# Attention and FFN on one core: scores of two heads at once on the two halves of the array's rows

## The chip, the cores and the metric

The kernel runs on one core of a Trainium2 chip. The metric is the device time of one execution in microseconds (us), taken as the median of several runs. Engines are named as in the profile: PE is TensorE (PEld its weight loads), DVE is VectorE, ACT is ScalarE, POOL is GpSimd, SP issues the DMAs of this kernel.

## The reference

The inputs are q, k and v of shape (4, 8, 576, 64) (batch, heads, sequence, head size), and the two weights of a feed-forward layer.

```python
q_rot, k_rot = rotate(q), rotate(k)                       # rotary embedding over the head size
scores = matmul(q_rot, k_rot^T) / sqrt(64)
attn = exp(scores - max(scores)) ; attn /= sum(attn) + 1e-9
x = (attn @ v), heads joined                               # 2304 tokens x 512
h = x @ w_in                                               # 512 -> 2048
out = (h * clip(h + 3, 0, 6) / 6) @ w_out                  # 2048 -> 512
```

The weights arrive as 64-bit floats and are decoded on the chip. The factors of the data are large, so the kernel keeps nearly the accuracy of f32: nearly every operand is split into a high and a low f16 part, and products are sums of several f16 matmuls.

## The kernel before, in words

**Tiles.** The 2304 tokens are 18 tiles of 128. A batch has 4.5 tiles, so tiles 4 and 13 are mixed: their upper 64 tokens belong to one batch and their lower 64 to the next (`BAT`, line 26). Tile 0 goes a way of its own in f32 (`attention_first`). For the other 17 tiles, each of the 8 heads is one unit `attention(i)` (line 637), with i = 8 t + h.

**One head.** `emit_qk` (line 600) computes 128 x 576 scores into a PSUM tile S of two banks (288 columns in each). There are two buffers of S. The q of a head lies in `qT` as 128 rows: 64 rows of the high part over 64 of the low part; k lies in `kT` in the same way. So one matmul over 128 rows gives high x high + low x low, and a second one, with a copy of q whose halves are swapped, gives the two cross products: two matmuls for each bank, four a head, with the full array. In a mixed tile each of these is two matmuls, one for each half of the tokens, on 64 columns of the array each (line 611). DVE then scales S in place and takes the maximum (line 655), ACT takes the exponential in place in S with the sum (line 657), ACT or DVE writes its high f16 part to P in SBUF (lines 664, 666), and DVE the low part (line 668). Only then is S free. A DMA transpose turns P into PT (line 674), and `emit_av` (line 614) multiplies PT with the parts of v, 14 matmuls of 64 columns. After the eight heads `emit_x` (line 818) normalises the tile, and a transpose hands it to the FFN (`ffn_h`, line 871, and `ffn_o`, line 937), which works on blocks of one or two tiles, with three f16 products for every f32 one.

**Preparation.** `prep_q` (line 340) loads a tile of q, bounds it (ACT or DVE), rotates it (lines 277 to 282, on POOL mostly), splits it into q1 (high and low of each head side by side; the low part is line 302), copies it with the halves swapped to q2 (line 357, DVE), and transposes both by DMA (lines 362 and 364). `prep_k` (line 377) and `prep_v` (line 443) do the like for a batch of keys and values. `decode_w` (line 520) turns 64-bit words of the weights into f32: one pass for the magnitude (line 528, ACT), one for the low word (line 541 on POOL, 543 on ACT), one for the sign (line 549 on ACT), one that joins them (line 555, DVE). `split_w_steps` splits the result.

**The order.** The order of every engine's instructions is written when the kernel is built. Each piece of work is a generator that yields what it needs next: an engine and an estimated time ("D" for DVE, "A", "P", "E" for PE), a DMA ("S" plain, "Z" transpose), a buffer ("R"), a condition ("C"). A small planner, `Emission` (line 41), keeps a clock of these estimates, gives each engine the waiting piece of the lowest priority number, and emits instructions in that order; on the chip each engine then runs its own list strictly in order. Some steps may go to one of several engines (`yield "Xeh", {...}`): the planner takes the cheapest by its clock and a bias. Small letters ("d") and "P" mark work that takes the port to SBUF that DVE and POOL share, by the planner's model. The dictionary `CFG` (line 38) holds the priorities and biases. Attention comes ahead of the FFN by priority, but `attn_ready` (line 758) holds a head back until enough FFN units are done (`lead`). The planner counts 0.5 us of PE for the scores of one head:

```python
yield "R", "S"
yield "E", 0.5
S = psum.tile([128, 2, 512], F32, tag="S", bufs=2, name="S")
emit_qk(i, S)
```

## Time and profile before

| | us |
|---|---|
| median of 3 runs | 659.03 |
| lowest and highest run | 657.67, 661.57 |
| the profiled execution, its own time | 654.6 |
| span of its instructions | 652.7 |

A page of the profile shows the busy time of each engine, the span in 40 slices and the groups of instructions; views of the trace answer for a stretch, a line or a tile. Busy PE is not PE at its peak: a matmul is shown from its start to its end, and matmuls in a row overlap, so the time that a matmul takes from its neighbours is read from the distance of starts, not from its length. In the timeline, instructions of one line in a row are merged to one row with its start and its count.

### The profile page before, as it was taken

How to read it: one execution, taken by the hardware profiler on the slowest of the kernel's cores; microseconds unless marked ns; L12 is line 12 of the kernel's file. 1: busy time of each engine (PE TensorE's matmuls, PEld its weight loads, DVE VectorE, ACT ScalarE, POOL GpSimd, SP SyncE). 2: the span in 40 equal slices, each digit the busy share in tenths (PEclk: the TensorE clock that was granted, in tenths of full speed). 3: DMA queues.
4: the chain of work that ended last, by engine and by line, in shares of the span. 5: the costliest groups of instructions: out<-in, count | busy, mean ns of one | idle time of the engine just before them, and what ended most of it. 6: DMA issues, size and time to landing. Idle time of an engine off the chain costs nothing.

```text
span 652.7 us, 14935 instructions
## 1 busy us (share of the span) xinstructions
PE 573.3 (88%) x5860; PEld 410.8 (63%) x5860; DVE 447.6 (69%) x844; ACT 386.2 (59%) x715; POOL 322.2 (49%) x363
## 2 busy tenths in 40 slices
PE   2478888468899999898998999999999999999997
PEld 1366764256576766675776756766677677666663
DVE  6899889999975986688697787765777656311010
ACT  4875988655775766667577667664667656312110
POOL 3574535597433795634499441562544524233330
PEclk9989799569999999999999999999999999999999
DMA  9995394976979998998996999777699756310000
GB/s 300 320 322 135 138 262 101 194 138 119 207 157 143 209 162 146 179 168 170 201 158 133 186 203 163 135 143 144 109 158 175 134 113 106 74 33 17 17 1 33
DMA packets 252294, 97.96 MB, mean 150 GB/s; under 512 B 235840, under 2 KB 235968, under 8 KB 252224
## 3 DMA queue, kind: packets, MB, share of 16 engines
q1 hardware_dynamic: 252224, 97.01, 73.5%
q8 instruction: 46, 0.75, 0.5%
q14 instruction: 24, 0.20, 0.1%
HBM read 31.97 MB, written 4.72 MB: 56 GB/s over the span
## 4 chain that ended last, share of the span: by engine, by line
PE 52%; POOL 14%; DVE 11%; DMA 9%; issue 7%; ACT 6%; SPq 1%; POOLq 0%; DVEq 0%; ACTq 0%
PE o L963 20%; PE h L901 17%; DMA PT<-P 6%; PE av L626 5%; PE S L608 5%; POOL ropeA L277 3%; POOL kst L280 3%; POOL kst L282 3%; DVE P L668 2%; DVE S L655 2%; PE S L697 2%; DVE tg L922 1%; PE S L611 1%; PE av L747 1%; DMA raw<-in_w_out 1%
## 5 line engine op out<-in xcount | busy, mean ns | idle before, releaser
L901 PEld LDWEIGHTS <-wi_st 128*128 128x128 f16 x1920 | 164.7, 98 | 55.3 <-issue 3.4
L963 PE MATMUL o<-wo_st,g 128*128 128x512 f16 x696 | 186.2, 379 | 2.8 <-ACT wo_st L983 1.6
L901 PE MATMUL h<-wi_st 128*128 128x256 f16 (+1 forms) x1344 | 162.3, 259 | 1.1 <-DVE tg L922 0.7
L657 ACT ACTIVATE S<-S,mx 128x576 f32<-128x576 f32 x136 | 96.9, 713 | 100.9 <-DVE S L655 99.1
L655 DVE TENSOR_SCALAR_CACHE_REDUCE S<-S,sig 128x576 f32<-128x576 f32 x136 | 109.6, 819 | 31.1 <-PE S L608 25.3
L668 DVE SCALAR_TENSOR_TENSOR P<-S,P 128x576 f16<-128x576 f32 x136 | 100.9, 752 | 31.7 <-ACT P L664 31.2
L294 POOL TENSOR_SCALAR g<-tg 128x512 f16<-128x512 f32 x44 | 28.0, 637 | 182.0 <-DVE tg L922 172.3
L922 DVE SCALAR_TENSOR_TENSOR tg<-tg,h 128x512 f32<-128x512 f32 x68 | 46.5, 683 | 89.3 <-ACT tg L915 89.3
L626 PEld LDWEIGHTS <-PT 128*128 128x128 f16 (+1 forms) x2128 | 74.2, 103 | 42.7 <-DMA PT<-P 26.1
L915 ACT ACTIVATE tg<-h,g,block_sc 128x512 f32<-128x512 f32 x68 | 52.8, 776 | 79.5 <-PE h L901 70.8
L963 PEld LDWEIGHTS <-g 128*128 128x128 f16 x696 | 64.9, 98 | 44.5 <-POOL g L932 6.9
L608 PE MATMUL S<-kT,qT 128*128 128x288 f16 x480 | 79.9, 297 | 13.4 <-DVE P L668 13.1
L664 ACT ACTIVATE P<-S 128x576 f16<-128x576 f32 x135 | 85.6, 647 | 1.8
L626 PE MATMUL av<-vA,PT 128*128 128x64 f16 (+1 forms) x1520 | 64.9, 197 | 21.1 <-DMA PT<-P 20.1
L932 POOL TENSOR_TENSOR g<-tg,g 128x512 f16<-128x512 f32 x58 | 67.4, 1162 | 8.8 <-ACT g L290 5.3
L901 PE MATMUL h<-xTa,wi_st 128*128 128x256 f16 (+1 forms) x576 | 68.4, 255 | 0.0
L608 PEld LDWEIGHTS <-qT 128*128 128x128 f16 x480 | 44.8, 101 | 33.7 <-DVE P L668 17.4
L626 PE MATMUL av<-vB,PT 128*128 128x64 f16 (+1 forms) x608 | 39.4, 196 | 0.0
L963 PE MATMUL o<-wo_st 128*128 128x512 f16 x120 | 32.7, 380 | 2.3 <-POOL wo_st L294 1.3
L277 POOL TENSOR_TENSOR ropeA<-kst,rope_sb 128x512 f32<-128x512 f32 (+1 forms) x16 | 20.9, 1308 | 13.7 <-DMA kst<-in_k 13.0
L841 POOL TENSOR_TENSOR x<-x,x 128x512 f16<-128x512 f32 x15 | 18.3, 1217 | 17.9 <-ACT x L290 17.9
L657 ACT ACTIVATION_READ_ACCUMULATOR S<-S,mx 128x1 f32 x136 | 26.6, 196 | 0.0
(150 smaller groups left out, 761.9 us busy)
## 6 DMA issues: line engine op xcount, KB each, us to landing
raw<-in_w_in SPq DMA_DIRECT2D x16, 512.0 KB, 7.6
raw<-in_w_out SPq DMA_DIRECT2D x16, 512.0 KB, 4.6
qraw<-in_q SPq DMA_DIRECT2D x18, 256.0 KB, 3.2
out<-wo_st SPq DMA_DIRECT2D x17, 256.0 KB, 2.6
kst<-in_k SPq DMA_DIRECT2D x16, 256.0 KB, 4.3
vst<-in_v SPq DMA_DIRECT2D x15, 256.0 KB, 4.5
PT<-P SPq DMA_TRANSPOSE x136, 3.4
vB<-vA SPq DMA_DIRECT2D x8, 256.0 KB, 3.9
```

What stands on the lines that cost most here:

```text
L277: ENG[e].tensor_tensor(out=v4(ta), in0=x4[:, :, ::-1, :], in1=sinb.to_broadcast([n, 8, 2, 32]), op=ALU.mult)
L608: PE.matmul(out=S[:, j, 0:288], lhsT=qT_t[t][:, o, h, :], rhs=kT_t[b0][:, h, ks], **st)
L626: PE.matmul(out=av[r0:r1, h, :], lhsT=PT[:, blk, r0:r1], rhs=rhs, start=(n == 0), stop=(n == len(terms) - 1))
L655: DVE.tensor_scalar(out=E, in0=E, scalar1=sig_t[t], scalar2=3.0e38, op0=ALU.mult, op1=ALU.min, accum_out=mx)
L657: ACT.activation(out=E, in_=E, func=ACTF.Exp, scale=-1.0, bias=mx, accum_out=sum_t[t][:, h:h + 1])
L664: ACT.activation(out=hi, in_=E, func=ACTF.Copy, scale=ES)
L668: DVE.scalar_tensor_tensor(out=lo, in0=E, scalar=ES, in1=hi, op0=ALU.mult, op1=ALU.subtract)
L901: PE.matmul(out=h[:, i, :], lhsT=wi_h(p, wl)[:, 256 * c + f0:256 * c + f0 + 128], rhs=xT[:, 4 * xl + c, :], start=(n == 0), stop=(n == 11))
L915: ACT.activation(out=tg, in_=hf, func=ACTF.Relu, scale=osc[j], bias=g3)
L922: DVE.scalar_tensor_tensor(out=whole if j < NF else tg, in0=tg, scalar=6.0 * GAM, in1=hf, op0=ALU.min, op1=ALU.mult)
L932: ENG[e].tensor_tensor(out=gf[:, 1], in0=tg, in1=gf[:, 0], op=ALU.subtract)
L963: PE.matmul(out=os[n][0], lhsT=g[:, gl, mm % nm, 128 * n:128 * n + 128], rhs=wo_h(mm, wl), start=(mm == 0 and gl == 0 and wl == 0), stop=( ...
```

## The change

- Scores are computed for two heads at once. q is now laid out as 512 columns of high parts and then 512 of low parts; its transpose `qT` has 8 slices of 128 rows: slices 0 to 3 are the high parts of two heads each (64 rows a head), slices 4 to 7 the low parts. k is laid out in the same way.
- For each pair of heads there are three terms (high x high, high x low, low x high) instead of four; each is a matmul over 64 rows, on the upper half of the array's rows for the even head and on the lower half for the odd one. The two heads write to the two S buffers, so a pair takes both at once.
- The swapped copy of q and its transpose fall away; q16 and qT have half the size, q16 one buffer.
- The exponential may go to a new SBUF tile E (two buffers). The planner decides for each head: if an E is free and the shared port is free soon enough (`CFG["sb"]` of the phase). S is then free after the exponential, and the two parts of P are made from E; the high part on DVE is then estimated at 0.44 us.
- The low word of the weights is read as 16-bit words (its upper half) instead of 32-bit ones, by the same two engines; the planner's estimate for ACT falls from 1.35 to 1.15 us.
- The bounds of v and of the first weight may go to ACT as well as to DVE.
- The planner's numbers in `CFG` are all new (among them `lead` 32 to 29, `a16` 1 to 0, `gate` 1.71 to 2.284).

```diff
-LOW = 2.0 ** -29 * (1 - 2.0 ** -10), -0.5 + 7.5 * 2.0 ** -10
+LOW = 2.0 ** -13, -0.5 + 2.0 ** -14
...
+NE = 2
...
-        q1 = left.tile([128, 8, 2, 64], F16, tag="q16", bufs=2, name="q1")
-        bound(e, am, x, q1.rearrange("p h a d -> p (h a d)")[:, 0:512])
+        q16 = left.tile([128, 2, 512], F16, tag="q16", name="q16")
+        bound(e, am, x, q16[:, 0])
...
-        x3 = x.rearrange("p (h d) -> p h d", d=64)
-        yield from split_steps(x3, s, q1[:, :, 0, :], q1[:, :, 1, :])
-        yield "d", 0.41
-        q2 = left.tile([128, 8, 2, 64], F16, tag="q16", bufs=2, name="q2")
-        DVE.tensor_copy(out=q2, in_=q1[:, :, ::-1, :])
+        yield from split_steps(x, s, q16[:, 0], q16[:, 1])
...
-        qT = left.tile([128, 2, 8, 128], F16, tag="qT", bufs=2, name="qT")
-        SP.dma_start_transpose(out=qT[:, 0], in_=q1.rearrange("p h a d -> p (h a d)"))
-        yield "Z", 0.9
-        SP.dma_start_transpose(out=qT[:, 1], in_=q2.rearrange("p h a d -> p (h a d)"))
+        qT = left.tile([128, 8, 128], F16, tag="qT", bufs=2, name="qT")
+        SP.dma_start_transpose(out=qT, in_=q16.rearrange("p l n -> p (l n)"))
...
-            yield from split_steps(x3, sc[0][0:n], k16[0:n, :, 0, :], k16[0:n, :, 1, :])
+            yield from split_steps(kst[0:n, i], sc[0][0:n], k16[0:n, 0:512], k16[0:n, 512:1024])
...
-                yield "D", 0.67
-                bound("D", am[:, i:i + 1], vst[:, i])
+                e = yield "Xvb", {"D": 0.67, "A": 0.82}
+                bound(e, am[:, i:i + 1], vst[:, i], vA[:, 1, i])
...
+        upper = raw.bitcast(U16)[:, :, 1]
-        e = yield "Xlow", {"P": 1.35, "A": 1.35}
+        e = yield "Xlow", {"P": 1.35, "A": 1.15}
         if e == "P":
-            POOL.tensor_scalar(out=low, in0=raw[:, :, 0], scalar1=LOW[0], scalar2=LOW[1], op0=ALU.mult, op1=ALU.add)
+            POOL.tensor_scalar(out=low, in0=upper, scalar1=LOW[0], scalar2=LOW[1], op0=ALU.mult, op1=ALU.add)
...
-        e = "D" if kind == "i" else em.choose("wbo", {"D": 1.21, "A": 1.25}, 3)
+        e = em.choose("wb" + kind, {"D": 1.21, "A": 1.25}, 3)
...
     def emit_qk(i, S):
-        t, h = divmod(i, 8)
+        t, c = i // 8, i % 8 // 2
         b0, b1 = BAT[t]
-        for o in range(2):
+        groups = [(0, 128, b0)] if b0 == b1 else [(0, 64, b0), (64, 128, b1)]
+        terms = (0, 0), (0, 4), (4, 0)
+        for n, (lq, lk) in enumerate(terms):
             for j in range(2):
-                ks = slice(288 * j, 288 * j + 288)
-                st = dict(start=(o == 0), stop=(o == 1))
-                if b0 == b1:
-                    PE.matmul(out=S[:, j, 0:288], lhsT=qT_t[t][:, o, h, :], rhs=kT_t[b0][:, h, ks], **st)
...
+                for p in range(2):
+                    d = slice(64 * p, 64 * p + 64)
+                    for r0, r1, b in groups:
+                        PE.matmul(out=S[p][r0:r1, j, 0:288], lhsT=qT_t[t][d, lq + c, r0:r1],
+                                  rhs=kT_t[b][d, lk + c, 288 * j:288 * j + 288],
+                                  start=(n == 0), stop=(n == len(terms) - 1))
...
-        yield "R", "S"
-        yield "E", 0.5
-        S = psum.tile([128, 2, 512], F32, tag="S", bufs=2, name="S")
-        emit_qk(i, S)
+        if h % 2 == 0:
+            yield "R", "S"
+            yield "R", "S"
+            yield "E", 0.76
+            for p in range(2):
+                S_t[i + p] = psum.tile([128, 2, 512], F32, tag="S", bufs=2, name="S")
+            emit_qk(i, (S_t[i], S_t[i + 1]))
...
+        else:
+            yield "C", lambda: i in qk_done
+        S = S_t.pop(i)
...
+        in_sbuf = em.tokens["E"] > 0 and em.port - em.clock < CFG["sb"][em.phase]
+        if in_sbuf:
+            yield "R", "E"
         yield "A", 0.93
-        ACT.activation(out=E, in_=E, func=ACTF.Exp, scale=-1.0, bias=mx, accum_out=sum_t[t][:, h:h + 1])
+        if in_sbuf:
+            E = left.tile([128, 576], F32, tag="E", bufs=NE, name="E").rearrange("p (j n) -> p j n", j=2)
+        ACT.activation(out=E, in_=S[:, :, 0:288], func=ACTF.Exp, scale=-1.0, bias=mx, accum_out=sum_t[t][:, h:h + 1])
         yield "N", 0.0
+        if in_sbuf:
+            free("S")
...
-        e = yield "Xeh", {"A": 0.65, "D": 0.75}
+        e = yield "Xeh", {"A": 0.68, "d": 0.44} if in_sbuf else {"A": 0.65, "D": 0.75}
...
-        yield "D", 0.75
+        yield "d" if in_sbuf else "D", 0.75
...
-        free("S")
+        free("E" if in_sbuf else "S")
...
-                and (i == 0 or i - 1 in started) and units_done[0] >= i - CFG["lead"]
+                and (i % 2 or i - 1 in started) and units_done[0] >= i - CFG["lead"]
```

## Rows read from the trace of the kernel before

**Rows 1.** The page: busy us, share of the span and instructions of each engine, and the busy tenths of TensorE and its granted clock in 40 slices of the span.
```profile
PE 573.3 (88%) x5860; PEld 410.8 (63%) x5860; DVE 447.6 (69%) x844; ACT 386.2 (59%) x715; POOL 322.2 (49%) x363
...
PE   2478888468899999898998999999999999999997
...
PEclk9989799569999999999999999999999999999999
```

**Rows 2.** Busy time by stretch: the stretch and its length in us, then the busy us and instructions of each engine, the granted clock of TensorE, the share of the DMA engines and GB/s.
```profile
60.00:100.00 40.00, 33.73 (x230) 27.64 (x231) 34.30 (x50) 33.47 (x48) 16.50 (x13) 0.87 0.75 208
100.00:170.00 70.00, 48.86 (x534) 34.31 (x533) 67.04 (x112) 48.29 (x86) 44.78 (x44) 0.78 0.75 136
...
170.00:570.00 400.00, 380.97 (x4419) 273.34 (x4417) 287.53 (x599) 251.61 (x500) 204.81 (x244) 1.00 0.85 155
...
570.00:637.00 67.00, 65.24 (x451) 43.44 (x449) 8.93 (x13) 12.67 (x17) 24.14 (x27) 1.00 0.06 17
637.00:652.70 15.70, 11.40 (x52) 4.99 (x52) 0.00 (x0) 1.37 (x2) 0.10 (x1) 1.00 0.09 34
```

**Rows 3.** Waits of TensorE's matmuls from 170 to 570 us: who waited for whom, us in total, times, longest us.
```profile
PE av L626 <- DMA PT<-P: 10.3, 11, 2.5
PE S L608 <- DVE P L668: 3.3, 5, 1.3
PE o L963 <- ACT wo_st L983: 1.6, 1, 1.6
```

**Rows 4.** The timeline of TensorE around the scores of two heads of an unmixed tile (full array): start in us, length to the end of the last one, line, operation, array rows x columns, shape, count.
```profile
387.72 0.81 PE L963 MATMUL o<-wo_st 128*128 128x512 f16 x3
388.36 1.14 PE L608 MATMUL S<-kT,qT 128*128 128x288 f16 x8
389.34 0.46 PE L626 MATMUL av<-vA,PT 128*128 128x64 f16 x10
```

**Rows 5.** The same around the scores of two heads of a mixed tile (halves of the array's columns).
```profile
195.72 0.81 PE L963 MATMUL o<-wo_st 128*128 128x512 f16 x3
196.46 1.17 PE L611 MATMUL S<-kT,qT 128*64 128x288 f16 x16
197.56 0.34 PE L901 MATMUL h<-wi_st 128*128 128x128 f16 x3
```

**Rows 6.** The same around the only matmuls of the kernel that use half of the array's rows (transposes of 64 keys in f32).
```profile
26.18 0.69 PE L320 MATMUL xt<-id_sb,kst 64*128 64x64 f32 x4 [6.43 <-DVE kst L282]
26.80 2.07 PE L697 MATMUL S<-wi_st,xTa 128*128 128x288 f32 x4
```

**Rows 7.** Score matmuls before and after 170 us, line 608 (full array) and then line 611 (halves of columns): stretch, length, busy us and count of the matmuls and of the weight loads, clock, DMA.
```profile
0.00:170.00 170.00, 18.66 (x92) 9.28 (x92) 0.87 0.80 201
170.00:653.00 483.00, 61.25 (x388) 35.52 (x388) 1.00 0.72 132
...
170.00:653.00 483.00, 10.47 (x128) 6.12 (x128) 1.00 0.72 132
```

**Rows 8.** The timeline of TensorE around the scores of single heads of a mixed tile.
```profile
187.42 0.68 PE L611 MATMUL S<-kT,qT 128*64 128x288 f16 x8 [0.23 <-DVE P L668]
188.03 0.68 PE L901 MATMUL h<-wi_st 128*128 128x128 f16 x9
188.75 0.68 PE L611 MATMUL S<-kT,qT 128*64 128x288 f16 x8
189.36 0.34 PE L901 MATMUL h<-wi_st 128*128 128x128 f16 x3
```

**Rows 9.** The tile q: line, engine and operation with count, duration in ns (min/median/max), first and last start in us, shapes. SPq is the queue that issues the DMAs.
```profile
L362 SPq DMA_TRANSPOSE qT<-q x17: 1232/1305/2063, 46.6 to 519.2; - x17
L357 DVE COPY q<-q x17: 409/420/823, 47.1 to 518.8; 128x1024 f16<-128x1024 f16 x17
L364 SPq DMA_TRANSPOSE qT<-q x17: 1322/1339/2657, 49.9 to 524.9; - x17
```

**Rows 10.** The tile S, with the same columns.
```profile
L655 DVE TENSOR_SCALAR_CACHE_REDUCE S<-S,sig x136: 804/820/828, 64.0 to 559.8; 128x576 f32<-128x576 f32 x136
L655 DVE DVE_READ_ACCUMULATOR S<-S,sig x136: 130/141/145, 64.8 to 560.6; 128x1 f32 x136
L657 ACT ACTIVATE S<-S,mx x136: 668/715/725, 71.9 to 560.7; 128x576 f32<-128x576 f32 x136
...
L668 DVE SCALAR_TENSOR_TENSOR P<-S,P x136: 739/751/759, 78.3 to 562.3; 128x576 f16<-128x576 f32 x136
L664 ACT ACTIVATE P<-S x135: 630/651/677, 73.3 to 561.6; 128x576 f16<-128x576 f32 x135
...
L712 ACT ACTIVATE E<-S,bi x8: 724/732/776, 31.0 to 60.4; 128x576 f32<-128x576 f32 x8
```

**Rows 11.** Line 302, the low split with both operands in SBUF, with the same columns.
```profile
L302 DVE SCALAR_TENSOR_TENSOR q<-qraw,qs,q x17: 732/752/1631, 45.8 to 518.0; 128x512 f16<-128x512 f32 x17
L302 DVE SCALAR_TENSOR_TENSOR k<-kst,ks,k x15: 736/1172/1748, 133.2 to 371.9; 128x512 f16<-128x512 f32 x12, 64x512 f16<-64x512 f32 x3
```

**Rows 12.** VectorE's costliest groups from 100 to 170 us: line, operation, shapes, count, busy us, mean ns, idle before in us.
```profile
L655 DVE TENSOR_SCALAR_CACHE_REDUCE S<-S,sig 128x576 f32<-128x576 f32 x17 | 13.7, 814 | 0.0
L668 DVE SCALAR_TENSOR_TENSOR P<-S,P 128x576 f16<-128x576 f32 x18 | 13.3, 748 | 0.7 <-ACT P L664 0.7
...
L357 DVE COPY q<-q 128x1024 f16<-128x1024 f16 x2 | 0.8, 418 | 0.0
```

**Rows 13.** Lines 541 (low words of the weights) and 549 (signs), with the columns of rows 9.
```profile
L541 POOL TENSOR_SCALAR wo_st<-raw x8: 1346/1422/2315, 16.5 to 57.2; 128x1024 uint16<-128x1024 uint32 x8
L541 POOL TENSOR_SCALAR tw<-raw x8: 1344/1358/1377, 64.4 to 97.3; 128x1024 uint16<-128x1024 uint32 x8
...
L549 ACT ACTIVATE tw<-raw x8: 1346/1364/1371, 69.5 to 101.2; 128x1024 f16<-128x1024 f32 x8
```

More of the change, by code (lines that the diff above doesn't have):

```diff
@@ L194, in attention_ffn @@
     TT = {"d": 0.68, "P": 1.265}
[L195 removed]
+    em = Emission({"S": 2, "E": NE, "P16": NP16, "PT": NPT, "av": 1, "x": 1, "h": 2, "tg": 2, "g": NG,
                    "o": 1, "ob": 1, "rope": 1, "rope0": 1, "k16": 1, "raw": 3, "raw1": NR1, "tw": 0, "tw0": 2, "rope1": 1})
@@ L417, in split @@
             n = N[i]
-            x3 = kst[0:n, i].rearrange("p (h d) -> p h d", d=64)
             if start is None:
                 yield "R", "k16"
-            k16 = left.tile([128, 8, 2, 64], F16, tag="k16", name="k16") if start is None else \
-                wo16[:, 8 + i].rearrange("p (h a d) -> p h a d", a=2, d=64)
-            yield from split_steps(x3, sc[0][0:n], k16[0:n, :, 0, :], k16[0:n, :, 1, :])
+            k16 = left.tile([128, 1024], F16, tag="k16", name="k16") if start is None else wo16[:, 8 + i]
+            yield from split_steps(kst[0:n, i], sc[0][0:n], k16[0:n, 0:512], k16[0:n, 512:1024])
             yield "Z", 0.9
             SP.dma_start_transpose(out=kT[0][:, :, 128 * i:128 * i + n],
-                                   in_=k16[0:n].rearrange("p h a d -> p (h a d)"))
+                                   in_=k16[0:n])
             yield "N", 0.0
@@ L538, in decode_w @@
         low, sign = h[:, :, 0].bitcast(U16), h[:, :, 1]
-        e = yield "Xlow", {"P": 1.35, "A": 1.35}
+        upper = raw.bitcast(U16)[:, :, 1]
+        e = yield "Xlow", {"P": 1.35, "A": 1.15}
         if e == "P":
-            POOL.tensor_scalar(out=low, in0=raw[:, :, 0], scalar1=LOW[0], scalar2=LOW[1], op0=ALU.mult, op1=ALU.add)
+            POOL.tensor_scalar(out=low, in0=upper, scalar1=LOW[0], scalar2=LOW[1], op0=ALU.mult, op1=ALU.add)
         else:
-            ACT.activation(out=low, in_=raw[:, :, 0], func=ACTF.Copy, scale=LOW[0], bias=LOW[1])
+            ACT.activation(out=low, in_=upper, func=ACTF.Copy, scale=LOW[0], bias=LOW[1])
         e = yield "Xsg", {"P": 1.34, "A": 1.15}
@@ L594, in split_w_steps @@
         wdone[kind] = done if kind == "i" else 2 * done + 1
[L597 removed]
+    PT_t, sum_t, av_t, S_t = {}, {}, {}, {}
     started, qk_done, done_av = set(), set(), set()
     def emit_qk(i, S):
[L601 removed]
+        t, c = i // 8, i % 8 // 2
         b0, b1 = BAT[t]
[L603 removed]
+        groups = [(0, 128, b0)] if b0 == b1 else [(0, 64, b0), (64, 128, b1)]
+        terms = (0, 0), (0, 4), (4, 0)
+        for n, (lq, lk) in enumerate(terms):
             for j in range(2):
[L605 to L612 removed]
+                for p in range(2):
[4 more added lines that the diff above has]
+                                  start=(n == 0), stop=(n == len(terms) - 1))
     def emit_av(i):
```

15 lines of the change are left out of this document (5 added, 10 removed).

## The prediction

> **What bounds the kernel now.** I read the page's shares first. TensorE is busy 88% of the span, VectorE 69%, and the slices show TensorE at 8 or 9 tenths from the tenth slice on [rows 1]. Because that share averages unlike stages, I next read the table by stage [rows 2]. Up to 170 us TensorE is far from full, and from 100 to 170 us VectorE is the bound: 67.04 of 70 us busy, while TensorE does 48.86 us at a mean clock of 0.78. From 170 to 570 us TensorE is busy 380.97 of 400 us at full clock, VectorE only 287.53, ScalarE 251.61, GpSimd 204.81. From there to the end TensorE still does 65.24 of 67 and 11.40 of 15.7 us. So after 170 us the time is TensorE's work plus about 19 us of idle before 570 us, and a microsecond taken from TensorE's work there comes off the end. The waits [rows 3] name that idle: 10.3 us for transposed exponentials (PT), 3.3 us for an S buffer that VectorE still reads. The forecast rests on this stage.
>
> **The array's time for scores.** A pair of heads is now 8 matmuls of 288 columns on the full array. Their first starts at 388.36 us and the next operation at 389.34, so a pair takes 0.98 us, 0.1225 us a matmul [rows 4]. The new pair is 12 matmuls of 64 rows. If the two halves of the rows run together, these are 6 slots of 0.1225, 0.735 us. No row shows two matmuls on row halves, but tiles 4 and 13, whose 128 tokens span two batches, run their scores on two halves of the *columns*. There 16 matmuls start at 196.46 and the next operation at 197.56 us: 1.10 us for 8 slots [rows 5], so halves of columns do run together, and the burst costs 0.12 us beyond 8 x 0.1225. Ahead of that burst, three matmuls on 512 columns take from 195.72 to 196.46, 0.74 us; ahead of the burst on the full array the same three take from 387.72 to 388.36, 0.64 us [rows 4, 5]. So going into the split form costs 0.10 us and coming out 0.12: 0.22 us a burst.
>
> I take this for row halves too. The nearest row on row halves is a group of four small f32 transposes on 64 rows, from 26.18 to 26.80 us, of which the merged line tells only that 0.62 us pass for four [rows 6]; it excludes neither a cost nor none. A pair is then 0.735 + 0.22 = 0.955 us, against 0.98. From 170 us on, 388 of the 480 full-array matmuls run, 97 heads or 48.5 pairs [rows 7]: 48.5 x 0.025 = **1.2 us saved**.
>
> All 128 split matmuls, 16 heads, also run after 170 us [rows 7]. A burst of 8 for one head takes 0.61 us (187.42 to 188.03, 188.75 to 189.36) [rows 8] and 0.10 us to enter: 16 x 0.71 = 11.4 us if each stood alone, 8 x 1.20 = 9.6 if all came in twos [rows 5]; I take 10.6. With four quarters at once, eight pairs cost 8 x 0.955 = 7.6: **3.0 us saved**. The sum for TensorE is 4.2 us. Its bounds: without any price for the change of form, 48.5 x 0.245 + 10.6 - 8 x 0.735 = 11.9 + 4.7 = 16.6 us saved; with halves that don't overlap, 12 x 0.1225 + 0.22 = 1.69 a pair, 48.5 x 0.71 = 34 us lost.
>
> The Trainium skill, "TensorEngine Tiling (Array Packing)", section Theoretical Speedup, gives up to 2x for a contraction of 64 or less, by which a pair would be 0.735 us and the sum 16.6 us; its Key Properties say that a change of tiling mode drains the engine, which speaks against a burst as short as this one. The rows on column halves agree with the drain, 0.22 us; on row halves no row decides, and I keep the drain.
>
> **The copy of q and its second transpose.** Removed are 17 copies on VectorE (420 ns median) and 17 transposes on the SP queue (1339 ns to issue), 22.8 us of that queue's time [rows 9]. After 170 us VectorE has slack, so the copy is worth nothing there; two of the copies lie in 100 to 170 us: 2 x 0.42 = 0.8 us. The queue passes 136 PT transposes, and the 10.3 us of waits for PT are where relief would show [rows 3]: between 0 and 10.3 us, and since 17 transposes go and the 136 PT ones stay, I take **1 us**. The waits for PT then go on, as the next thing late. The new layout of q16 and k16 moves no work: the splits write as many elements. q16 has one buffer in place of two, but a tile's preparation starts when the scores of the tile before are nearly done, long after its transpose, so nothing waits for it.
>
> **Exponentials in SBUF.** S now comes free after the exponential instead of after both split passes; today it is held for those, 651 + 751 ns more [rows 10]. But a pair takes both S buffers at once, so its scores wait for the later of two. The 3.3 us of waits for S can vanish or grow; I take no change (the rival below has the other price). The exponential itself moves from PSUM to SBUF: the eight of the first tile that already write to SBUF take 732 ns against 715 [rows 10], 17 ns more on ScalarE, which is 63% busy from 170 to 570 us: nothing. The low split on VectorE now reads two operands from SBUF. From PSUM it took 739 to 759 ns in all 136 cases [rows 10]; the like operation with both operands in SBUF has medians of 752 (q) and 1172 (k) and goes up to 1748 [rows 11]. So it can be held up while GpSimd works. SBUF is chosen by the planner's guess that the shared port is free, so I take q's median, nothing. At k's median it is 0.42 us a head: the 18 low splits from 100 to 170 us [rows 12], where VectorE is full, would cost 7.6 us; later its slack covers it.
>
> The Trainium skill, "SBUF — State Buffer", section Who interferes with whom, says that a VectorE instruction with two SBUF inputs contends with GpSimd's reads, which speaks against this part; the spread of the rows agrees. The page gives no time for this shape.
>
> **The weights' low words.** The 16 passes stand on GpSimd today (1422 and 1358 ns medians, all before 100 us) [rows 13]. Reading 16-bit words instead of 32-bit moves as many elements; GpSimd is busy 16.50 of 40 us from 60 to 100 us [rows 2], so I cost it at nothing, 2 us either way. Should they move to ScalarE, the sign pass of the same shape takes 1364 ns there [rows 13], and ScalarE is 33.47 of 40 us busy: it would be late next.
>
> **The new planner numbers** change the order of everything. The order can't be read from this profile; TensorE's idle after 170 us, 19 us, bounds what a better one gives. I take nothing, with 8 us better and 8 worse as the ends.
>
> **Sum.** -4.2 - 1 - 0.8 = -6.0 us. The profiled execution took 654.6 us (span 652.7), so 648.6; the median of the runs is 659.03, 4.4 us above that execution, and on this footing the forecast is **653.0 us**, 0.9% faster. About 0.5%, 3.3 us, is what a measurement of this kernel can tell from no change.
>
> **Rivals.**
> *The change of form is free, or hidden* (chance 0.25). Scores then give 16.6 us, 12.4 more than I took: 640.6 us. For it: no row shows row halves draining. Against it: both directions of the column halves do.
> *Scores wait for two buffers* (slower, 0.17). QK of a pair can't start until the second head has left its buffer, one reduction and its read (820 + 141 ns) after the first [rows 10]. TensorE takes its work in a written order, so everything behind, FFN too, waits, and VectorE, which waits for the scores, gets them late. It was held five times for 0.66 us [rows 3]. If one pair in three of the 56.5 waits 0.66 us, that is 12.4 us against 6.0 saved: 665.4 us. It decides the sign from 0.11 us a pair on average. For it: these waits exist with single buffers. Against it: S is released earlier when the exponential goes to SBUF.
> *The halves don't run together* (0.06). 34 us lost on plain pairs; in mixed tiles 12 slots of column pairs, 1.69 - 1.33 = 0.36 x 8 = 3 us more: 659.03 + 37 - 1.8 = 694 us. Against it: column halves do.
> *It comes out even* (0.13): another order gives back the 4 to 8 us; 658 us.
> The forecast itself has 0.39.
>
> **Range and chances.** The first rival sets the lower end, with about 3 us for fewer PT waits: 637. The second sets the upper end, with the even case inside: 668. Left out are the third rival, a stall on more pairs, and the better order on top of the free change, together about 0.2. Of the forecast's 0.39 I put 0.04 within 0.5%, for a planner order that gives back half. Faster by over 0.5% is then 0.35 + 0.25 = 0.60, within 0.5% 0.13 + 0.04 = 0.17, slower 0.17 + 0.06 = 0.23.
>
> **What would show it.** The new profile should have 912 score matmuls of half the rows (60 pairs of 12, 8 of 24), two and two starting together, and bursts of about 0.85 us with 0.10 before them; busy TensorE after 170 us down by about 4 us; no copy of q; 17 q transposes; waits for S about as long as now. A burst of 0.74 us with no gap would make the first rival right, one of 1.5 the third, and S waits of over 10 us after 170 us the second. The forecast would be wrong if TensorE's idle after 170 us left 11 to 27 us, or if TensorE filled up much earlier or later than at 170 us.

## The result, and the profile after

The changed kernel takes **666.25 us** (median of 10 runs, 660.98 to 669.17) against 658.55 us for the kernel before in the same runs: 1.011 times as long, with a 95% interval of 1.0082 to 1.0137. It is slower by 7.7 us where 6.0 us less was forecast. The profiled execution took 663.26 us, its span is 661.4.

The page of the changed kernel, busy us, share of the span and instructions of each engine, and the slices of TensorE and its clock, answers to [rows 1]:
```profile
PE 574.2 (87%) x6164; PEld 396.4 (60%) x6164; DVE 449.5 (68%) x827; ACT 386.5 (58%) x716; POOL 337.5 (51%) x360
...
PE   1578876597899858979999898999999999999996
...
PEclk9998997589999986979999998999999999999999
```
TensorE, VectorE and ScalarE are busy as long as before (within 2 us), GpSimd 15 us longer. The span grew by 8.7 us, and TensorE's idle time from 652.7 - 573.3 = 79.4 to 661.4 - 574.2 = 87.2 us. So the time is lost in waiting. The stages show where, with the columns of [rows 2]:
```profile
100.00:170.00 70.00, 52.28 (x597) 35.61 (x597) 64.01 (x108) 45.64 (x81) 47.00 (x45) 0.80 0.68 122
170.00:300.00 130.00, 109.67 (x1529) 76.81 (x1527) 95.08 (x199) 78.57 (x160) 69.22 (x75) 0.91 0.84 160
300.00:450.00 150.00, 141.26 (x1556) 95.94 (x1553) 115.35 (x230) 96.51 (x192) 84.33 (x90) 0.99 0.80 149
...
170.00:570.00 400.00, 370.33 (x4511) 254.20 (x4509) 290.11 (x585) 247.39 (x494) 206.16 (x230) 0.97 0.78 145
```
The same view of the kernel before, for the two stretches that [rows 2] give only within 170 to 570 us:
```profile
170.00:300.00 130.00, 119.17 (x1568) 87.06 (x1565) 100.59 (x215) 84.84 (x168) 74.59 (x86) 1.00 0.94 171
300.00:450.00 150.00, 142.40 (x1563) 100.75 (x1561) 113.45 (x236) 97.89 (x195) 82.42 (x97) 1.00 0.88 164
```
From 100 to 170 us TensorE now does 3.4 us more than before. From 170 to 300 us it idles 20.3 us in place of 10.8, and its granted clock there is 0.91 in place of 1.00: part of what it does, it does at half its clock (from 242 to 259 us the granted clock is 0.50). What it waits for after 170 us, as in [rows 3]:
```profile
PE av L622 <- DMA PT<-P: 14.5, 11, 4.0
PE S L606 <- DVE P L679: 12.2, 11, 5.3
```
The waits for PT were 10.3 us and are 14.5; those for an S buffer were 3.3 and are 12.2. Two single waits make 9.3 us of these: 5.27 us for S, which ends at 245.50 us, and 3.98 us for PT, which ends at 290.70.

The first of them, in the timeline of TensorE (the bracket is the idle time before, and what ended it):
```profile
235.71 0.91 PE L606 MATMUL S<-kT,qT 64*128 64x288 f16 x12
236.55 1.47 PE L974 MATMUL o<-wo_st,g 128*128 128x512 f16 x6
...
245.50 0.42 PE L606 MATMUL S<-kT,qT 64*128 64x288 f16 x1 [5.27 <-DVE P L679]
246.16 1.62 PE L606 MATMUL S<-kT,qT 64*128 64x288 f16 x11 [0.24 <-DVE P L679]
```
and in that of VectorE, over the same time:
```profile
237.52 0.82 DVE L656 TENSOR_SCALAR_CACHE_REDUCE S<-S,sig 128x576 f32<-128x576 f32 x1
238.25 0.14 DVE L656 DVE_READ_ACCUMULATOR S<-S,sig 128x1 f32 x1
240.47 1.00 DVE L304 SCALAR_TENSOR_TENSOR k<-kst,ks,k 128x512 f16<-128x512 f32 x1 [2.07 <-ACT k L292]
241.39 1.25 DVE L838 TENSOR_SCALAR rsum<-sums 128x8 f32<-128x8 f32 x1
242.68 0.20 DVE L839 RECIPROCAL rsum<-rsum 128x8 f32<-128x8 f32 x1
242.92 1.06 DVE L843 TENSOR_SCALAR rsum<-rsum,ra 128x8 f32<-128x8 f32 x1
244.08 0.69 DVE L845 TENSOR_TENSOR x<-av,rsum 128x512 f32<-128x512 f32 x1
244.69 1.41 DVE L679 SCALAR_TENSOR_TENSOR P<-S,P 128x576 f16<-128x576 f32 x2
```
TensorE wants both S buffers, and these are held until the two low splits at 244.69. Those stand in VectorE's written order behind a split of k, which waits 2.07 us for ScalarE, and behind two operations on 8 columns that take 1.25 and 1.06 us here where the medians of their lines in this trace are 0.166 and 0.231. GpSimd was rotating k without a pause all that time, the last of it
```profile
241.00 1.62 POOL L279 TENSOR_TENSOR ropeA<-kst,rope_sb 64x512 f32<-64x512 f32 x1
242.70 1.25 POOL L282 TENSOR_TENSOR kst<-kst,rope_sb 64x512 f32<-64x512 f32 x1
244.03 1.26 POOL L284 TENSOR_TENSOR kst<-kst,ropeA 64x512 f32<-64x512 f32 x1
```
in its own timeline, each of them beside one of the slow operations of VectorE or the one after it.

Three of the costliest groups, GpSimd's low part of the FFN's gated values (`g`, the gate below) and VectorE's low split from PSUM (`P<-S,P`) and from SBUF (`P<-E,P`), with busy us, mean ns and idle before:
```profile
L943 POOL TENSOR_TENSOR g<-tg,g 128x512 f16<-128x512 f32 x59 | 75.0, 1272 | 59.1 <-ACT g L292 56.2
...
L679 DVE SCALAR_TENSOR_TENSOR P<-S,P 128x576 f16<-128x576 f32 x82 | 60.4, 752 | 27.3 <-ACT P L675 27.1
...
L679 DVE SCALAR_TENSOR_TENSOR P<-E,P 128x576 f16<-128x576 f32 x54 | 50.9, 954 | 14.0 <-ACT P L675 13.7
```
54 of 136 heads wrote their exponentials to SBUF. Their low splits take 954 ns in the mean against 752 from PSUM; the median is 758 and the longest takes 1823 ns, where the longest of before took 759 [rows 10]. The gate takes 1272 ns in the mean, and in the kernel before it took 1162:
```profile
L932 POOL TENSOR_TENSOR g<-tg,g 128x512 f16<-128x512 f32 x58 | 67.4, 1162 | 8.8 <-ACT g L290 5.3
```
VectorE's busy time still grew by only 1.9 us, because the 17 copies of q (7 us at their median [rows 9]) are gone.

### The profile page after: what moved, and what is told of

It is laid out like the page before. It is cut to its first block, busy times and chain, and to the rows that moved or that the text cites. A ratio compares the mean times of both kernels' runs of the same rounds, so it can differ in the third digit from the quotient of the medians.

```text
span 661.4 us, 15417 instructions
## 1 busy us (share of the span) xinstructions
PE 574.2 (87%) x6164; PEld 396.4 (60%) x6164; DVE 449.5 (68%) x827; ACT 386.5 (58%) x716; POOL 337.5 (51%) x360
## 4 chain that ended last, share of the span: by engine, by line
PE 56%; DVE 17%; DMA 9%; ACT 7%; issue 5%; SPq 2%; POOL 2%; POOLq 0%; DVEq 0%; ACTq 0%
PE o L974 20%; PE h L912 19%; PE S L606 7%; DMA PT<-P 6%; PE av L622 6%; DVE S L656 3%; DVE P L679 3%; DVE wo_st L304 1%; ACT S L666 1%; DVE vA L304 1%; PE S L708 1%; SPq L445 1%; DMA kst<-in_k 1%; DVE wi_st L550 1%; DMA raw<-in_w_in 1%
## 5 line engine op out<-in xcount | busy, mean ns | idle before, releaser
L943 POOL TENSOR_TENSOR g<-tg,g 128x512 f16<-128x512 f32 x59 | 75.0, 1272 | 59.1 <-ACT g L292 56.2
L606 PE MATMUL S<-kT,qT 64*128 64x288 f16 (+1 forms) x912 | 72.8, 299 | 22.8 <-DVE P L679 20.1
L296 POOL TENSOR_SCALAR g<-tg 128x512 f16<-128x512 f32 x36 | 23.1, 642 | 127.9 <-DVE tg L933 119.3
L666 ACT ACTIVATE S<-S,mx 128x576 f32<-128x576 f32 x82 | 58.3, 712 | 49.3 <-DVE S L656 47.6
L622 PE MATMUL av<-vA,PT 128*128 128x64 f16 (+1 forms) x1520 | 65.2, 197 | 24.8 <-DMA PT<-P 23.8
L679 DVE SCALAR_TENSOR_TENSOR P<-S,P 128x576 f16<-128x576 f32 x82 | 60.4, 752 | 27.3 <-ACT P L675 27.1
L606 PEld LDWEIGHTS <-qT 64*128 64x128 f16 (+1 forms) x912 | 39.7, 100 | 49.7 <-DVE P L679 21.0
L666 ACT ACTIVATE E<-S,mx 128x576 f32<-128x576 f32 x54 | 39.8, 739 | 40.7 <-DVE S L656 35.9
L679 DVE SCALAR_TENSOR_TENSOR P<-E,P 128x576 f16<-128x576 f32 x54 | 50.9, 954 | 14.0 <-ACT P L675 13.7
L675 ACT ACTIVATE P<-S 128x576 f16<-128x576 f32 x80 | 50.0, 646 | 0.9
L675 ACT ACTIVATE P<-E 128x576 f16<-128x576 f32 x45 | 29.6, 677 | 0.4
```

The source lines that it names most:

```text
L296: POOL.tensor_scalar(out=out, in0=in_, scalar1=s, scalar2=0.0, op0=ALU.mult, op1=ALU.add)
L606: PE.matmul(out=S[p][r0:r1, j, 0:288], lhsT=qT_t[t][d, lq + c, r0:r1], rhs=kT_t[b][d, lk + c, 288 * j:288 * j + 288], start=(n == 0), stop ...
L622: PE.matmul(out=av[r0:r1, h, :], lhsT=PT[:, blk, r0:r1], rhs=rhs, start=(n == 0), stop=(n == len(terms) - 1))
L666: ACT.activation(out=E, in_=S[:, :, 0:288], func=ACTF.Exp, scale=-1.0, bias=mx, accum_out=sum_t[t][:, h:h + 1])
L675: ACT.activation(out=hi, in_=E, func=ACTF.Copy, scale=ES)
L679: DVE.scalar_tensor_tensor(out=lo, in0=E, scalar=ES, in1=hi, op0=ALU.mult, op1=ALU.subtract)
```

## Experiments

Four theories stood against each other. **T1**: a pair's scores wait for two S buffers. **T2**: the written order, which the new planner numbers made, is worse on the chip. **T3**: low splits from SBUF are held up by GpSimd and make VectorE late. **T4**: the form on row halves costs TensorE more than the full array. "Order kept" below means that every engine's instructions stand in the sequence of the kernel named; otherwise the planner wrote a new one. The ratio behind each time is to the kernel before, run beside it, with its 95% interval; times of different runs are compared by these ratios as well as by their medians. Some runs leave work out and tell only what that work costs.

### The planner numbers exchanged

a_cfgB is the changed kernel with the numbers of before; b_cfgA is the kernel before with the new ones.
```diff
-CFG = {'a0': -1.15, 'a1': 3.714, ...
+CFG = {'a0': -0.441, 'a1': 2.342, ... 'sb': [0.1, 1, -0.3]}
```


> The changed kernel with the planner numbers of the kernel before. Theory 1 (a pair of heads must wait for both S buffers; this costs whatever the order): still slower than before, 662 to 670 us, TensorE's waits for S after 170 us 8 us or more. Theory 2 (only the new planner numbers are worse): 648 to 656 us, waits for S about 3 us. Theory 3 (the low split from SBUF is held up by GpSimd and makes VectorE late): 660 to 668 us, with the low split from E over 900 ns on average.

Measured: 679.78 us, 1.0358 [1.0324, 1.0393], above the range of every theory. TensorE waits 4.6 us for S from 170 to 570 us, where T1 named 8 or more; the low splits from SBUF take 999 ns in the mean, as T3 named.

> The kernel before with the planner numbers of the changed kernel, nothing else. Theory 1: 656 to 662 us, as before. Theory 2: 663 to 670 us, with TensorE's idle from 170 to 570 us near the changed kernel's 30 us. Theory 3: as before.

Measured: 674.07 us, 1.0262 [1.023, 1.0293]. This too is above every range; T2's is the nearest, and TensorE's idle from 170 to 570 us is 33.3 us. Each structure is 2 to 3% slower with the numbers made for the other than with its own. That planner numbers alone, which set the order and which engine does a step, move the time by 17 us is shown (b_cfgA against the kernel before), but not which part of the change needs which order.

### Pairs on the full array, and no exponentials in SBUF

b_pairtok adds one thing to the kernel before, two heads' scores issued together once both S buffers are free, and the planner writes a new order for it.
```diff
-        yield "R", "S"
-        yield "E", 0.5
...
+        if h % 2 == 0:
+            yield "R", "S"
+            yield "R", "S"
+            yield "E", 1.0
...
```


> The kernel before, with its four full-array matmuls a head, but the scores of two heads issued together once both S buffers are free. Theory 1: 664 to 672 us, waits for S after 170 us of 10 us or more against 3.3. Theories 2 and 3: 656 to 662 us.

Measured: 691.26 us, 1.0529 [1.0481, 1.0577]; from 170 to 300 us TensorE is busy 98.53 us at a clock of 0.88, and from 170 to 570 us it waits 13.4 us for S and 16.5 for PT. a_noE is the changed kernel with no buffer for exponentials in SBUF.
```diff
-NE = 2
+NE = 0
```


> The changed kernel with no exponential in SBUF (NE = 0), so S is held until the low split of each head. Theory 1: worse, 668 to 680 us, since both buffers come free later. Theory 2: within 3 us of the changed kernel's 666. Theory 3: better, 658 to 663 us.

Measured: 678.23 us, 1.0319 [1.029, 1.0349]; waits for S 16.8 us, for PT 13.9. T1 has the waits of b_pairtok and the time of a_noE right, while b_pairtok's time lies far above its 664 to 672 us; T3's forecast fails, since without exponentials in SBUF a_noE should have been faster than the changed kernel. Both have an order of their own, so neither is a pure price. Both are slower than the changed kernel, so the runs hold no version of pairs that gained by leaving that part out.

### The copy and the second transpose of q alone

b_nocopy is the kernel before, order kept, without the copy and the transpose of it. Both score matmuls read the unswapped q, so the cross products are left out: the run tells only what the copy and its transpose cost.
```diff
-        DVE.tensor_copy(out=q2, in_=q1[:, :, ::-1, :])
...
-        SP.dma_start_transpose(out=qT[:, 1], in_=q2.rearrange("p h a d -> p (h a d)"))
...
-                    PE.matmul(out=S[:, j, 0:288], lhsT=qT_t[t][:, o, h, :], rhs=kT_t[b0][:, h, ks], **st)
+                    PE.matmul(out=S[:, j, 0:288], lhsT=qT_t[t][:, 0, h, :], rhs=kT_t[b0][:, h, ks], **st)
```


> The kernel before with its written order kept, but without the swapped copy of q and its second transpose (both passes read the unswapped q, so the cross products are left out). All theories: the copy and the transpose are worth little, 1 to 3 us faster than before, at most a wait or two for PT fewer. If they were worth more than 5 us, the change lost more elsewhere than is thought.

Measured: 653.71 us, 0.9914 [0.988, 0.9949]. The kernel before took 657.37 us beside it, so the gain is 3.7 us by the medians and 5.7 by the ratio (3.4 to 7.9 by its interval). Waits of TensorE from 170 to 570 us:
```profile
PE S L605 <- DVE P L665: 5.2, 7, 2.0
PE av L623 <- DMA PT<-P: 5.0, 6, 2.8
```
Those for PT fell from 10.3 to 5.0 us, those for S grew from 3.3 to 5.2. The two profiled executions lie only 0.7 us apart (654.6 and 653.9 us), so where the gain of the medians lies can't be read from them. This part of the change gains two to three times the 1.8 us that were forecast for it.

### The full array in the new order

a_full keeps the changed kernel's order and its S buffers, and replaces a pair's 12 matmuls of 64 rows by 8 of 128 rows.
```diff
-        for n, (lq, lk) in enumerate(terms):
...
+        for p in range(2):
+            for n in range(2):
...
-                        PE.matmul(out=S[p][r0:r1, j, 0:288], lhsT=qT_t[t][d, lq + c, r0:r1],
...
+                        PE.matmul(out=S[p][r0:r1, j, 0:288], lhsT=qT_t[t][:, 4 * n + c, r0:r1],
```


> The changed kernel with its written order kept, but the scores of a pair on the full array, four matmuls of 128 rows a head, the even head first (the products mix two heads). It undoes the split form of the array alone; the pair still takes both S buffers. Theory 1 (waiting for two buffers): within 0.5% of the changed kernel, and the long wait for S near 240 us is still there. Rival (the split form costs more than its rows show, by draining the array at every burst): faster than the changed kernel by 4 us or more.

Measured: 665.76 us, 1.0121 [1.0082, 1.016], the changed kernel's time. The long wait is there, with the full array:
```profile
241.56 0.28 PE L619 MATMUL av<-vB,PT 128*128 128x64 f16 x4
247.04 2.10 PE L604 MATMUL S<-kT,qT 128*128 128x288 f16 x8 [5.20 <-DVE P L676]
```
T4 falls: the form on row halves costs nothing that the end shows. By the ratios a_full is 0.7 us slower than the changed kernel, and the two intervals leave about 3 us either way: the 4.2 us that were forecast for the form lie outside, a smaller gain can't be told from none.

### The planner told the pair's true price, or given more buffers

The planner takes a pair's burst for 0.76 us; it takes 0.95. a_E95 tells it so. a_sbE writes every exponential to SBUF for which a buffer is free.
```diff
-            yield "E", 0.76
+            yield "E", 0.95
```
```diff
- ... 'sb': [0.1, 1, -0.3]}
+ ... 'sb': [9, 9, 9]}
```


> The changed kernel with the planner told 0.95 us for the scores of a pair, which the trace shows, in place of 0.76. Theory 2 (the written order is the loss, since it was made with wrong prices): faster than the changed kernel, 655 to 662 us. Theory 1: another order, but the same kind of waits, 663 to 672 us.

Measured: 672.03 us, 1.022 [1.0163, 1.0276].

> The changed kernel with the exponential in SBUF whenever one of its two buffers is free, whatever the shared port does. Theory 1: S comes free earlier, waits for S after 170 us below 6 us, 656 to 664 us. Theory 3 (the low split from SBUF held up by GpSimd): the low split's mean from E rises from 954 ns to over 1000, VectorE late, 668 us or more.

Measured: 674.92 us, 1.0248 [1.0199, 1.0297], with 132 heads in SBUF at 1015 ns a low split, as T3 named. T2's forecast for a_E95 and T1's time for a_sbE fail. Neither mends it; both change the order, so neither says why.

### More exponentials in SBUF in the new order

a_forceE keeps the order and moves the other 82 heads to SBUF.
```diff
-        if in_sbuf:
+        moved = in_sbuf or live[0] < NE
+        live[0] += moved
+        if moved:
             E = left.tile([128, 576], F32, tag="E", bufs=NE, name="E").rearrange("p (j n) -> p j n", j=2)
...
+        live[0] -= moved
```


> The changed kernel with its written order kept; more heads write their exponential to SBUF: wherever fewer than two of the SBUF tiles are in use at that point of the order, also where the planner had left it in PSUM. Theory 1 (pairs wait for S, held until the low splits): TensorE's wait of 5.3 us for S near 245 us falls below 2 us, its waits for S after 170 us fall from 12 to under 6 us, and the time to 655 to 661 us. Theory 2 (the order alone): the order is the same, so within 0.5% of 666. Theory 3 (low splits from SBUF held up by GpSimd): slower than the changed kernel, more low splits over 900 ns.

Measured: 674.31 us, 1.0233 [1.0171, 1.0295], some 8 us above the changed kernel. Waits of TensorE from 170 to 570 us:
```profile
PE av L623 <- DMA PT<-P: 24.4, 10, 8.5
PE o L978 <- POOL g L947: 6.2, 7, 1.3
...
PE S L607 <- ACT E L669: 2.2, 2, 2.0
```
S comes free early and TensorE hardly waits for it; but 136 low splits of 1036 ns make VectorE busy 478 us in place of 449.5, PT comes later, and GpSimd's gates come late as well. T3's forecast holds. With most of the waits for S gone the kernel is slower, so these waits are not all of the cause; what S alone is worth this run can't say, since it also moves 82 heads to SBUF.

### Orders searched anew

a_re and a_re2 (pairs at 0.95 us) and b_re (the kernel before) have planner numbers searched for the earliest end by the planner's own account; only `CFG` differs.

> The changed kernel with the planner told 0.95 us for a pair's scores and new planner numbers for which its own clock ends earliest. Theory 2 (the loss lies in an order written for a price of 0.76 us): 650 to 658 us, no slower than before. Theory 1 (pairs cost whatever the order): 662 us or more.

Measured: 674.68 us, 1.022 [1.0157, 1.0283], 118 heads in SBUF at 991 ns; T2's forecast fails.

> The kernel before with new planner numbers found in the same way, prices as they were. It shows what another such order is worth to the structure before: by both theories 650 to 662 us. If it falls to 652 or less, before had slack of its own in the order; if it rises over 665, orders alone move the time by over 1% and the comparison of the two structures hangs on the order.

Measured: **652.59 us**, 0.9894 [0.9838, 0.995]: this version beats both kernels.

> As a_re, from another start: the same price of 0.95 us, other planner numbers. Theory 2: within 1% of a_re and 650 to 660 us. Theory 1: 662 us or more again. If a_re and a_re2 differ by over 1%, the order is what decides between them.

Measured: 684.44 us, 1.0384 [1.0316, 1.0453], 124 heads in SBUF at 1065 ns. T2 alone is unlikely: pairs with exponentials in SBUF took 666 to 684 us in the six orders that the planner wrote for them (the changed kernel, a_cfgB, a_E95, a_sbE, a_re, a_re2), and no search brought them under 666, while single heads took 652.6 to 674 in three. The ranges overlap, and a_re and a_re2 differ by 1.4% by their order alone.

### Two or four S tiles

To have more S buffers, scores of only 512 keys are computed (the last 64 are left out), so that an S tile is one bank; orders are kept. Two and four tiles, for both structures.
```diff
-                S_t[i + p] = psum.tile([128, 2, 512], F32, tag="S", bufs=2, name="S")
+                S_t[i + p] = psum.tile([128, 512], F32, tag="S", bufs=4, name="S")
```


> The changed kernel with its written order kept and 512 keys a head in place of 576 (the last 64 are left out), so that a tile of S is one PSUM bank; two S tiles, as now. It is the control for the next run: some us faster than the changed kernel, since every step of a head is a ninth shorter, with waits for S of about 12 us after 170 us still there.

Measured: 645.64 us, 0.9831 [0.9779, 0.9883].

> The same with four S tiles, nothing else changed. Theory 1 (a pair waits for both S tiles): 7 us or more faster than with two, waits for S after 170 us below 2 us, no stretch of half clock near 245 us. Theory 2 (the order) and theory 3 (the low split from SBUF): within 3 us of two S tiles, since order and low splits are the same.

Measured: 645.42 us, 0.9807 [0.9749, 0.9866].

> The kernel before, order kept, 512 keys, two S tiles of one bank: the control for the next run, some us faster than before.

Measured: 643.80 us, 0.9795 [0.9754, 0.9836].

> The same with four S tiles. With single heads the waits for S are 3 us after 170 us, so theory 1 gives 0 to 4 us faster than with two; 7 us or more would say that S is as dear with single heads as with pairs, and the pairs are not the cause.

Measured: 644.46 us, 0.9800 [0.9755, 0.9845]. Waits of TensorE from 170 to 570 us, first a_k512_2:
```profile
PE av L620 <- DMA PT<-P: 11.8, 9, 2.3
PE S L605 <- DVE P L677: 9.6, 6, 5.6
```
and a_k512_4:
```profile
PE av L620 <- DMA PT<-P: 18.8, 7, 7.9
PE o L969 <- POOL g L939: 2.7, 4, 0.9
```
With four tiles no matmul waits for S, and the time is the same: the 5.6 us for S turn into 7.9 us for PT at the same place, and from 245.8 us on the clock is still halved for 10 us. T1's forecast of 7 us or more fails: VectorE is late, and S is only the first place where TensorE meets that. But with 512 keys the changed structure is only 1.8 us slower than the old one (0.4% by the ratios, inside their intervals), though here too each of its 54 low splits from SBUF takes 0.23 us more in the mean than one from PSUM (911 against 685 ns). By the medians most of the 7.7 us is thus gone before a tile is added, and what more S tiles would be worth with 576 keys is not shown.

### Exponentials in SBUF in the old order

b_nocopy_fE is b_nocopy with every exponential in SBUF. To make room, q16 has one buffer in place of two (as in the changed kernel) and qT half the size; in the trace no instruction on q waits for that buffer. The order is that of the kernel before, with single heads and the full array.
```diff
-        q1 = left.tile([128, 8, 2, 64], F16, tag="q16", bufs=2, name="q1")
+        q1 = left.tile([128, 8, 2, 64], F16, tag="q16", bufs=1, name="q1")
...
-        ACT.activation(out=E, in_=E, func=ACTF.Exp, scale=-1.0, bias=mx, accum_out=sum_t[t][:, h:h + 1])
+        E = left.tile([128, 576], F32, tag="E", bufs=2, name="E").rearrange("p (j n) -> p j n", j=2)
+        ACT.activation(out=E, in_=S[:, :, 0:288], func=ACTF.Exp, scale=-1.0, bias=mx, ...)
```


> The kernel before without the copy of q and its second transpose (b_nocopy, 653.7 us), in its own order, and with one thing added: every exponential of tiles 1 to 17 is written to a tile of SBUF, so all 136 low splits read two operands from SBUF. The cross products are left out, as in b_nocopy. If low splits from SBUF are what makes VectorE late (they took 0.95 to 1.06 us there against 0.75 from PSUM), 136 of them cost VectorE 27 to 40 us, much of it beside other work: the time goes up by 6 to 12 us to 660 to 666 us, the waits for PT after 170 us grow from 5 us to over 10. If they cost only under the new written order, the time stays at 653 to 656 us and the waits at about 5.

Measured: 677.47 us, 1.0294 [1.0239, 1.0349], against 0.9914 for b_nocopy: **23.8 us** by the medians, 25 by the ratios, twice the most that was expected. The stretch from 300 to 450 us, first in b_nocopy and then in b_nocopy_fE (columns of [rows 2]):
```profile
300.00:450.00 150.00, 144.57 (x1567) 102.41 (x1568) 111.92 (x233) 98.40 (x196) 82.86 (x98) 0.99 0.83 157
```
```profile
300.00:450.00 150.00, 134.18 (x1385) 95.53 (x1385) 123.65 (x225) 96.89 (x191) 85.46 (x83) 0.99 0.76 149
```
The low split's group in b_nocopy_fE (busy us, mean ns, idle before), and its longest waits of TensorE from 170 to 570 us:
```profile
L666 DVE SCALAR_TENSOR_TENSOR P<-E,P 128x576 f16<-128x576 f32 x136 | 139.1, 1033 | 31.6 <-ACT P L662 31.0
```
```profile
PE o L961 <- POOL g L930: 10.4, 11, 2.7
PE av L623 <- DMA PT<-P: 6.4, 6, 2.3
```
From 300 to 450 us VectorE does fewer instructions in more busy time, and TensorE falls 10.4 us behind, though VectorE is only 82% busy; from 170 to 300 us it falls another 5.2 behind with VectorE 81% busy. GpSimd is held up as well: its busy time grows from 321.7 to 358.0 us, VectorE's from 440.5 to 482.6. TensorE's waits for GpSimd's gates grow from 1.4 to 10.4 us, those for PT only from 5.0 to 6.4, where over 10 were expected. GpSimd's line 294, the high part of the gates, takes 770 ns in the mean against 629. So the cost is shown, and by these waits it reaches TensorE at least as much through GpSimd's lateness as through VectorE's.

### GpSimd's rotations left out

a_norope keeps the changed kernel's order and leaves out GpSimd's rotation passes of q (from tile 1) and of k (from the second batch).
```diff
+        kept = start is not None or e == "D"
...
+        if kept:
+            ENG[e].tensor_tensor(out=x4, in0=x4, in1=cosb, op=ALU.mult)
...
```


> The changed kernel in its own order, with GpSimd's rotation passes of q (from tile 1 on) and of k (from the second batch on) left out, so q and k are not rotated. If VectorE is late because it shares with GpSimd (theory of the port), the low splits from SBUF fall from 0.95 to about 0.75 us, the small operations that took 1.3 us near 241 us fall to some 0.2, the 5.27 us wait for S near 245 us shrinks to under 1 us, and the time falls by 8 to 12 us to 654 to 658 us. If the written order itself makes VectorE late, the low splits still take 0.95 us or the wait near 245 us stays at 4 us or more, and the time stays at 663 to 668 us.

Measured: 651.03 us, 0.9897 [0.9845, 0.9949], 14 us below the changed kernel by the ratios and 15 by the medians, more than expected and not all in the way expected. VectorE's timeline at the place of the long wait:
```profile
233.87 0.75 DVE L308 SCALAR_TENSOR_TENSOR k<-kst,ks,k 128x512 f16<-128x512 f32 x1 [2.07 <-ACT k L296]
234.53 0.17 DVE L842 TENSOR_SCALAR rsum<-sums 128x8 f32<-128x8 f32 x1
234.74 0.20 DVE L843 RECIPROCAL rsum<-rsum 128x8 f32<-128x8 f32 x1
234.97 0.23 DVE L847 TENSOR_SCALAR rsum<-rsum,ra 128x8 f32<-128x8 f32 x1
...
235.92 1.41 DVE L683 SCALAR_TENSOR_TENSOR P<-S,P 128x576 f16<-128x576 f32 x2
```
and TensorE's:
```profile
236.72 0.29 PE L610 MATMUL S<-kT,qT 64*128 64x288 f16 x1 [2.81 <-DVE P L683]
```
The same chain takes 2.2 us less, just what GpSimd had cost it: 1.00 to 0.75, 1.25 to 0.17 and 1.06 to 0.23 us. The 2.07 us for ScalarE stay, and the wait falls to 2.81 us, not to under 1: that rest is the written order's. The SBUF low splits fall to a mean of 863 ns, not 750; GpSimd still has its gates. The waits for PT did not shrink (17.3 us after 170 us), and 6.7 us of the gain were there before 182 us: the av matmuls that wait for PT at 181.53 us in the changed kernel stand at 174.81 here. So GpSimd's work beside VectorE costs the changed kernel time in several places. That it costs this kernel more than the one before is not shown by this run, since the rotations were not taken out of that one; q and k also come earlier without them.

## Why the prediction was wrong

**What bounds the kernel.** "A microsecond taken from TensorE's work there comes off the end" failed. After 170 us TensorE was busy 95% of the time [rows 2], but what fills it comes through VectorE, GpSimd, SP's queue and the written order: its idle time there grew from 19 to 29.7 us and its clock fell from 1.00 to 0.97. a_full does the scores on the full array in the same order and takes the same time within the noise.

**The array's time for scores** was right as a price. A burst of a mixed tile in the timeline of the changed kernel, and one of a plain tile behind three matmuls on 512 columns:
```profile
461.81 0.93 PE L606 MATMUL S<-kT,qT 64*64 64x288 f16 x24
462.67 0.51 PE L622 MATMUL av<-vA,PT 128*64 128x64 f16 x20
...
466.82 0.81 PE L974 MATMUL o<-wo_st,g 128*128 128x512 f16 x3
467.57 0.91 PE L606 MATMUL S<-kT,qT 64*128 64x288 f16 x12
468.41 0.50 PE L912 MATMUL h<-wi_st 128*128 128x256 f16 x3
```
The plain pair takes 0.84 us and the three before it 0.75, against 0.98 and 0.64 on the full array [rows 4]: 0.03 us saved a pair in this one burst, 0.025 forecast. The mixed pair takes 0.86 us here, 1.10 after a wait at 196.12 us, and before it took 1.10 [rows 5]. Row halves run together and pay for the change of form like column halves. The rivals of a free form and of halves that don't overlap fall. The Trainium skill, "TensorEngine Tiling (Array Packing)", section Key Properties, says that a switch of tiling mode drains the engine; the 0.11 us on the way in and as much on the way out agree. The up to 2x of its section Theoretical Speedup does not appear at bursts of this length: 0.84 us against 0.98.

**The copy of q and its second transpose**: the direction was right and the size wrong: 3.7 to 5.7 us where the sum had 1 + 0.8. The waits for PT fell as forecast, though the profiled execution shows hardly any of the gain. The prediction had the bound (0 to 10.3 us) and took its low end because 136 transposes stay.

**Exponentials in SBUF** is the step that failed. "I take q's median, nothing", and at k's price "later its slack covers it". The mean is 954 ns, 0.20 us above PSUM's, 54 x 0.20 = 10.9 us of VectorE; and the slack did not cover it. In b_nocopy_fE 136 heads cost 23.8 us, and TensorE fell 15.6 of them behind from 170 to 450 us, where VectorE was 82% busy. A median hid the price: it is 758 ns, and the mean carries the splits that were held up. VectorE works in a fixed sequence, so a late low split delays all that stands behind it; and GpSimd, whose busy time grew by 36 us, is held up too, and with it the gates that TensorE waits for. An estimate from that run, 54/136 of 23.8, is 9.4 us for the changed kernel; a_forceE's 8 us for 82 heads would make it 5.3. No run takes these 54 back to PSUM with the changed kernel's order kept, so their price in it stays an estimate. The Trainium skill, "SBUF — State Buffer", section Who interferes with whom, says that a VectorE instruction with two SBUF inputs contends with GpSimd's reads. The prediction quoted it, named 7.6 us as the price at k's median and put nothing in the sum; the runs agree with the page: with GpSimd's rotations left out the mean falls from 954 to 863 ns.

**The weights' low words**: 15 of 16 stayed on GpSimd, with medians of 1355 ns (`wo_st`) and 1462 (`tw`) against 1422 and 1358 [rows 13]. No run tests them alone; nothing points to them.

**The new planner numbers**: "I take nothing, with 8 us better and 8 worse". Orders moved either structure by 17 us or more (b_cfgA against the kernel before, a_re2 against the changed kernel), so the bound was too narrow. With -3.7 to -5.7 for the copy, +5.3 to +9.4 for SBUF and nothing for the array, the sum is -0.4 to +5.7 us against the 7.7 measured. By this estimate 2 to 8 us are left for the pairs and their order; b_pairtok and a_noE say that pairs cost without SBUF, but each came with an order of its own, and no run issues pairs with the old order kept, so the two could not be told apart and that part of the cause stays open.

**The rivals.** "Scores wait for two buffers" gave 665.4 us and named S waits of over 10 us; 666.25 and 12.2 us were measured, where the forecast took the waits for S as unchanged. That fit is no proof: with 512 keys four S tiles took the waits away and left the time, and a_forceE took most of them away and was slower. The wait may still be part of the 2 to 8 us that stay open. A number and a sign can fit a mechanism that does not decide.

**Its test** for being wrong, an idle TensorE outside 11 to 27 us from 170 to 570 us, did say so: 400 - 370.33 = 29.7.

## What to carry to other kernels

A buffer moved from PSUM to SBUF to be released early is paid for by the engine that reads it next: price the operation by the mean of a like row with both operands in SBUF, not by its median, and count the engine on the other side too. When a wait grows, give its waiter what it lacks before calling it the cause; if the same lateness comes back under another name, look at the engine that both names share. And in a kernel with a written order, change one part with the order kept before searching a new order for all of it: here leaving out the copy alone gained 3.7 to 5.7 us, and the whole change lost 7.7.

## What the runs showed that was not expected

- Two operations of VectorE on 8 columns took 1.25 and 1.06 us (medians 0.166 and 0.231) while GpSimd worked without a pause, and 0.17 and 0.23 us with GpSimd's rotations left out.
- From 170 to 300 us the granted clock is 0.91 in the changed kernel (0.88 in b_pairtok), where the kernel before had 1.00. From 242 to 259 us, around the long wait and shorter ones behind it, it is 0.50, the lower of the two clock levels, 1.2 GHz: eleven matmuls of a score burst take 1.62 us there, where a whole burst of twelve takes 0.91 at 467.57 us. So a wait costs more than its own length.
- With 512 keys in place of 576 the changed structure loses 1.8 us and not 7.7 against the old one by the medians (0.4% by the ratios, whose intervals are 0.4 to 0.5% either way), with the same 54 heads in SBUF. No run says why.
